# Attention scores by rows in every second unit, with P turned by the DMA and V as the matmul weights

## The chip, the cores and the metric

The kernel runs on one core of one Trainium2 chip. The metric is the time of one execution on the device in microseconds; below it is given as the median of several runs. The profile is of one further execution, taken by the hardware profiler.

## What is computed

One transformer layer over 2048 tokens of width 512: a modulated layer norm, attention with 32 query heads over 8 cached key/value heads (2048 keys, head size 128, four query heads to a key head), an output projection with a gate, and then a gMLP block with a spatial mixing matrix. The part that matters here is the attention:

```python
q = (x @ wq).reshape(B, Sq, Hq, Dh).transpose(0, 2, 1, 3)
k = jnp.repeat(k_cache, rep, axis=1)
v = jnp.repeat(v_cache, rep, axis=1)
scores = jnp.einsum('bhqd,bhkd->bhqk', q, k) * Dh ** (-0.5)
p = softmax(scores, axis=-1)
o = jnp.einsum('bhqk,bhkd->bhqd', p, v)
return o.transpose(0, 2, 1, 3).reshape(B, Sq, Hq * Dh) @ wo
```

The block after it computes `z = gelu(h @ w_in)`, normalises its second half, mixes it over tokens with `w_sp`, multiplies with the first half and projects with `w_out`.

## The kernel before

**Units.** The attention is cut into 128 units. A unit is one key head (a group `g`) and one tile of 128 queries, with the four query heads of that group together: 512 query rows against 2048 keys. There are 8 groups of 16 units. The order of all work is written out by hand: the main loop runs over iterations `it`, each of 8 slots, and in iteration `it` the scores of unit `it`, P times V of unit `it - 1` and the output projection of unit `it - 3` are interleaved slot by slot. A piece of work can be hung on a slot with `at(it, slot, fn)`, and the query projections are spread over slots through the dictionary `fill`. Each engine runs its instructions in the order in which this loop emits them.

**Scores by columns (`qk`, line 965).** A slot takes two blocks of 128 keys. For each, a block of transposed keys is the weight of the matmul, and the 512 query rows are streamed, so the scores come out with keys on the partitions and queries along the free axis. Two such matmuls of 512 columns fill one tile `s_ps` (two PSUM banks; there are two such tiles). One ScalarE instruction takes the exponential of the 1024 columns and writes bf16 into `pTs[u]`, which already is P transposed. No maximum is subtracted; a range check on the reciprocals in `rall` at the end guards a second, general path.

**P times V (`pv`, line 987).** For each query head and each of 16 key blocks the tile of P transposed (128 x 128) is the weight, and V with a column of ones beside it (129 columns) is streamed. So a unit has 64 matmuls of 129 columns, and the column of ones gives the sum of the row. After two heads VectorE takes the reciprocal (line 1006) and multiplies it in (line 1007, `onorm`). At the end of the unit SyncE's queue issues a DMA transpose of `onorm` into `oT` (line 1015), two iterations ahead of the output projection that reads it.

**Output projection and query projection.** `wo_proj` (line 1019) has four matmuls of 512 columns per unit and adds the result to an accumulator `xacc` on VectorE. `qproj` (line 928) has 16 matmuls of 512 columns for four units; four land in the slots of each unit.

**Loads and the rest.** GpSimd's queue loads V, `wq`, `wo`, the second part of the modulation weights (`wmod_b`, which lies in the buffer `wsp`) and `w_in` (`win_sb`). SyncE's queue issues all DMA transposes: keys of the next group (line 739), `oT`, the normalised inputs, and tiles of the spatial matrix (`load_wsp`, line 1102), of which the first 16 are spread over the attention and 48 come after it. The modulation columns and rows (`mod_cols_b`, `mod_rows`) are computed in iterations 9 and 10. After the last unit come the gMLP's projections (lines 1182 and 1221), the spatial mix (line 1336) and the last projection (line 1357).

Of the kernel before, what the change touches and what calls it, by code (L numbers as in the profile page):

```python
# [575 lines left out]
def kernel(  # L576
# [76 lines left out]
    mv2 = res.tile([P, NT, nc.vector.BN_AGGR_DIM], FP32, name="mv2")  # L653
    mvz = res.tile([P, NT, nc.vector.BN_AGGR_DIM], FP32, name="mvz")
    mhalf = res.tile([P, CT], FP32, name="mhalf")
    win_sb = res.tile([P, NDT, F], BF16, name="win_sb")
    wmod_a = res.tile([P, NDT, 2 * D], BF16, name="wmod_a")
    wmod_b = wspp.tile([P, NDT * 4 * D], BF16, name="wsp")[:].rearrange(
        "p (k n) -> p k n", k=NDT
    )  # L660
# [3 lines left out]
    def bank(name):  # L664
        return psum.tile([P, 512], FP32, name=name)
# [259 lines left out]
        )  # L925
    warm(2)

    def qproj(b, heads, c0, n):

        g, ch = divmod(b, NCH)  # L930
        if b not in qTs:
            qTs[b] = early.tile([P, REP, 512], BF16, name="qT")
        one = n * len(heads) <= 512
        ps = {}

        def mm(hh, dt):
            if dt == 0 and (not one or hh == heads[0]):
                ps[0] = bank("misc")
            o0 = (hh - heads[0]) * n if one else 0
            nc.tensor.matmul(  # L940
                ps[0][:, o0 : o0 + n],
                lhsT=wqs[g][:, dt, hh * DH : (hh + 1) * DH],
                rhs=hTs[ch][:, dt, c0 : c0 + n],
                start=(dt == 0),
                stop=(dt == NDT - 1),
            )
            if dt == NDT - 1 and (not one or hh == heads[-1]):
                hs = heads if one else [hh]
                dst = qTs[b][:, hs[0] : hs[-1] + 1, c0 : c0 + n]
                src = ps[0][:, 0 : len(hs) * n].rearrange("p (h q) -> p h q", q=n)  # L950
                nc.vector.tensor_copy(out=dst, in_=src)  # L951

        return [lambda hh=hh, dt=dt: mm(hh, dt) for hh in heads for dt in range(NDT)]
# [2 lines left out]


    NU = HKV * NT
    pTs, onorms, oTs, xaccs, o_pss, h2Ts = {}, {}, {}, {}, {}, {}
    later = {}  # L960

    def at(it, slot, fn):
# [2 lines left out]
    def qk(u, i):  # L965
        g, j = divmod(u, NT)
        b, jj = g * NCH + j // CT, j % CT
        if i == 0:
            pTs[u] = late.tile([P, NKT, 512], BF16, name="pT")
        s_ps = bank2()  # L970
        for h in range(2):
            kt = 2 * i + h
            nc.tensor.matmul(  # L973
                s_ps[:, h * 512 : (h + 1) * 512].rearrange("p (r q) -> p r q", r=REP),
                lhsT=groups[g]["kT"][:, kt * P : (kt + 1) * P],
                rhs=qTs[b][:, :, jj * P : (jj + 1) * P],
                start=True,
                stop=True,
            )
        nc.scalar.activation(  # L980
            out=pTs[u][:, 2 * i : 2 * i + 2, :],
            in_=s_ps[:].rearrange("p (k q) -> p k q", k=2),
            func=ACT.Exp,
            scale=inv_sqrt_dh,
        )

    def pv(u, i):
        g = u // NT
# [152 lines left out]
    ln1_at(1, (0, 7), (1, 2), (2, 2))  # L1141
    ln1_at(2, (2, 4), (3, 1), (4, 5))
    ln1_at(3, (5, 1), (5, 5), (7, 4))
    at(2, 5, lambda: nc.gpsimd.dma_start(out=wmod_b, in_=wmod_dram[:, :, 2 * D : NMOD]))
    at(5, 5, lambda: nc.gpsimd.dma_start(out=win_sb[:], in_=win_dram))
    at(9, 4, mod_cols_b)
    at(10, 4, mod_rows)

    def set_fill(b):

        fs = qproj(b, list(range(REP)), 0, 512)
        for k, fn in enumerate(fs):
            it, slot = (b - 1) * CT + k // NDT, k % NDT
            if b == 1:
                it, slot = 2 + (10 + k) // 16, (5 + k // 2) % 8
            elif b == 2:
                it, slot = (5, k // 2) if k < 8 else (it, slot)
            fill.setdefault((it, slot), []).append(fn)

    def wsp0():  # L1160
        wsp[0] = wspp.tile([P, NT, 512], BF16, name="wsp")

    at(20, 0, wsp0)
    for st in range(NT):
        at(21 + 6 * st, 2, lambda st=st: load_wsp(wsp[0], 0, st))
    for g in range(1, HKV):
        it = (g - 1) * NT
        at(it + 7, 6, lambda g=g: load_k(g))
        at(it + 8, 3, lambda g=g: load_v(g))
        at(it + 9, 3, lambda g=g: load_wo(g, nc.gpsimd))  # L1170
        at(it + 7, 3, lambda g=g: load_wq(g, nc.gpsimd))


    zs = {}
# [81 lines left out]
    for ch in range(3):  # L1256
        at(NU + 5, 5 + ch, lambda ch=ch: z2_norm(ch))

    for it in range(NU + 6):
        if it < NU:  # L1260
            if it % CT == 0 and it // CT + 1 < NB:
                set_fill(it // CT + 1)
        elif it == NU:
            free_a.close()
            z2p = fast.enter_context(tc.tile_pool(name="z2p", bufs=1))
            zs["z2"] = z2p.tile([P, NT, FH], BF16, name="z2")
        wf = wo_proj(it - 3) if 3 <= it < NU + 3 else []
        for i in range(NSLOT):
            for fn in later.pop((it, i), []):
                fn()  # L1270
            if it < NU:
                qk(it, i)
            if 1 <= it <= NU:
                pv(it - 1, i)
            for fn in fill.pop((it, i), []):
                fn()
            if i >= 4 and wf:
                wf[i - 4]()
            if it >= NU:
                zrun(3)  # L1280
        if 3 <= it < NU + 3 and it - 3 >= (HKV - 1) * NT:
            ln2(it, (it - 3) % NT)
        if it == NU + 2:
            free_b.close()
            mlp = fast.enter_context(tc.tile_pool(name="mlp", bufs=1, side="right"))
# [170 lines left out]
```

## Time and profile before

| | |
|---|---|
| median of 10 runs | 1321.15 us (1320.66 to 1321.62) |
| the profiled execution, its own time | 1320.8 us |
| span of its profile | 1319.0 us |
| TensorE busy | 1311.5 us (99%) |
| ScalarE busy | 1077.7 us (82%) |
| VectorE busy | 471.7 us (36%) |
| attention units | about us 11 to 1144 of the span |
| after the units | about us 1144 to 1319 |

Busy time of an engine is the time in which at least one of its instructions is in progress. TensorE's matmuls overlap one another in their pipeline, so the mean duration of one matmul is longer than the distance between two, and what a matmul costs is read from the distance between starts. ScalarE's instructions can overlap a little too. The span is what the profiler saw of the instructions; the 1.8 us between it and the execution's own time lie around it.

### The profile page before, as it was taken

To read this page: it belongs to the slowest core of one execution; us is meant where nothing else is said; L and a number is where in the kernel's file an instruction comes from. 1 tells how busy PE (TensorE), PEld (TensorE's weight loads), DVE (VectorE), ACT (ScalarE), POOL (GpSimd) and SP (SyncE) were. 2 spreads that over 40 slices of the span, in tenths; PEclk is the share of its full clock that TensorE was granted. 3 is DMA by queue.
4 is the path that set the end of the run, shared out by engine and by line. 5 is a ranking of instruction groups with operands and counts; after the bars stand their busy time and mean duration, and the time that the engine had idled before them with its cause. 6 is when DMAs were issued, how large, how long until landed. Compare 5 with 4: busy or idle time off the path is not lost.

```text
span 1319.0 us, 27930 instructions
## 1 busy us (share of the span) xinstructions
PE 1311.5 (99%) x12359; PEld 858.3 (65%) x12359; DVE 471.7 (36%) x1162; ACT 1077.7 (82%) x1061; POOL 51.9 (4%) x96
## 2 busy tenths in 40 slices
PE   9999999999999999999999999999999999999998
PEld 5666666666666666666666666666666666644445
DVE  6532222222222222222222222222222566794444
ACT  7898999999999999999999999999999999650000
POOL 1201000000000000000000000000000000020000
PEclk9999999999999999999999999999999999999999
DMA  6542121112101111211110211121101122143300
GB/s 180 152 93 45 28 39 37 37 17 50 37 17 37 30 37 37 33 33 38 33 38 13 53 38 33 17 53 26 29 13 21 25 32 32 33 115 81 69 20 26
DMA packets 148944, 58.64 MB, mean 44 GB/s; under 512 B 138480, under 2 KB 144880, under 8 KB 148816
## 3 DMA queue, kind: packets, MB, share of 16 engines
q1 hardware_dynamic: 141792, 37.65, 15.5%
q0 software_dynamic: 4432, 16.91, 4.6%
q8 instruction: 98, 1.61, 0.5%
q10 hardware_dynamic: 2592, 2.23, 0.5%
q14 instruction: 30, 0.25, 0.1%
HBM read 21.89 MB, written 2.10 MB: 18 GB/s over the span
## 4 chain that ended last, share of the span: by engine, by line
PE 99%; DMA 0%; DVE 0%; ACT 0%; issue 0%; DVEq 0%
PE o_ps L995 35%; PE s_ps L973 33%; PE misc L1027 8%; PE misc L940 8%; PE misc L1336 7%; PE s_ps L1182 2%; PE s_ps L1221 2%; PE o_ps L1357 1%; PE s_ps L1357 1%; DMA wmod_a<-in_w_mod_dram 0%; PE misc L850 0%; PE o_ps L781 0%; DVE hT L809 0%; PE misc L1344 0%; ACT pT L980 0%; DVE tmp L1369 0%
## 5 line engine op out<-in xcount | busy, mean ns | idle before, releaser
L980 ACT ACTIVATE pT<-s_ps 128x1024 bf16<-128x1024 f32 x1024 | 1044.4, 1025 | 81.3 <-PE s_ps L973 7.1
L995 PEld LDWEIGHTS <-pT 128*128 128x128 bf16 x8192 | 548.5, 98 | 241.2
L995 PE MATMUL o_ps<-v,pT 128*128 128x129 bf16 x8192 | 631.4, 220 | 0.0
L973 PE MATMUL s_ps<-qT,kT 128*128 128x512 bf16 x2048 | 608.9, 379 | 0.3 <-ACT pT L980 0.2
L1006 DVE RECIPROCAL rall<-o_ps 128x2 f32<-128x2 f32 x256 | 43.7, 171 | 743.7 <-PE o_ps L995 740.4
L973 PEld LDWEIGHTS <-kT 128*128 128x128 bf16 x2048 | 199.3, 98 | 119.2 <-issue 0.8
L1027 PE MATMUL misc<-wo_g,oT 128*128 128x512 bf16 x512 | 194.0, 379 | 0.0
L940 PE MATMUL misc<-hT,wq_g 128*128 128x512 bf16 (+2 forms) x528 | 190.7, 371 | 0.1
L1007 DVE TENSOR_TENSOR onorm<-o_ps,rall 128x256 bf16<-128x256 f32 x256 | 108.7, 425 | 8.8
L1336 PE MATMUL misc<-wsp,z 128*128 128x512 bf16 (+2 forms) x560 | 100.7, 336 | 0.0
L951 DVE CAST qT<-misc 128x512 bf16<-128x512 f32 x127 | 86.4, 681 | 2.0 <-PE misc L940 2.0
L1336 PEld LDWEIGHTS <-z 128*128 128x128 bf16 x560 | 50.6, 98 | 48.5
L1040 DVE TENSOR_TENSOR xacc<-misc,xacc 128x512 f32<-128x512 f32 x112 | 76.2, 680 | 0.0
L940 PEld LDWEIGHTS <-wq_g 128*128 128x128 bf16 x528 | 50.4, 98 | 1.2 <-issue 0.4
L1027 PEld LDWEIGHTS <-oT 128*128 128x128 bf16 x512 | 50.1, 98 | 0.9
L1351 DVE TENSOR_TENSOR gb<-misc,bsp_bc 128x512 bf16<-128x512 f32 (+1 forms) x28 | 18.4, 658 | 58.3 <-PE misc L1336 58.3
L1182 PE MATMUL s_ps<-win_sb,hT 128*128 128x448 bf16 x128 | 27.0, 352 | 0.0
L1192 ACT ACTIVATE z<-s_ps 128x896 bf16<-128x896 f32 x16 | 14.7, 917 | 14.9 <-PE s_ps L1182 14.9
L1221 PE MATMUL s_ps<-hT,win_sb 128*128 128x512 bf16 x112 | 24.5, 379 | 0.0
L1229 ACT ACTIVATE z1T<-s_ps 128x1024 bf16<-128x1024 f32 x14 | 14.3, 1024 | 10.1 <-PE s_ps L1221 9.1
L692 DVE BATCH_NORM_STATS2 bnst<-x_sb 128x6 f32<-128x512 bf16 x32 | 21.9, 683 | 1.3 <-DMA x_sb<-in_A_x_dram 0.8
L1357 PE MATMUL o_ps<-wout_sb,yT 128*128 128x512 bf16 x84 | 20.1, 379 | 0.0
(88 smaller groups left out, 268.7 us busy)
## 6 DMA issues: line engine op xcount, KB each, us to landing
wq_g<-in_A_wq_dram POOLq DMA_DIRECT2D x7, 512.0 KB, 4.0
v<-in_A_v_cache_dram POOLq DMA_DIRECT2D x7, 512.0 KB, 5.9
wo_g<-in_A_wo_dram POOLq DMA_DIRECT2D x7, 512.0 KB, 4.7
oT<-onorm SPq DMA_TRANSPOSE x128, 2.4
wsp<-in_w_mod_dram POOLq DMA_DIRECT2D x1, 2048.0 KB, 8.8
out_dram<-yout ACTq DMA_DIRECT2D x16, 128.0 KB, 1.7
win_sb<-in_B_w_in_dram POOLq DMA_DIRECT2D x1, 1792.0 KB, 7.7
x_sb<-in_A_x_dram SPq DMA_DIRECT2D x3, 512.0 KB, 5.4
```

Source lines behind the costliest of these rows:

```text
L940: nc.tensor.matmul(ps[0][:, o0 : o0 + n], lhsT=wqs[g][:, dt, hh * DH : (hh + 1) * DH], rhs=hTs[ch][:, dt, c0 : c0 + n], start=(dt == 0), s ...
L951: nc.vector.tensor_copy(out=dst, in_=src)
L973: nc.tensor.matmul(s_ps[:, h * 512 : (h + 1) * 512].rearrange("p (r q) -> p r q", r=REP), lhsT=groups[g]["kT"][:, kt * P : (kt + 1) * P], ...
L980: nc.scalar.activation(out=pTs[u][:, 2 * i : 2 * i + 2, :], in_=s_ps[:].rearrange("p (k q) -> p k q", k=2), func=ACT.Exp, scale=inv_sqrt_dh,)
L995: nc.tensor.matmul(o_ps[:, hh % 2, 0 : DH + 1], lhsT=pTs[u][:, kt, hh * P : (hh + 1) * P], rhs=groups[g]["v1"][:, kt, 0 : DH + 1], start=( ...
L1007: nc.vector.tensor_tensor(out=onorms[u][:, hh - 1 : hh + 1, :], in0=o_ps[:, :, 0:DH], in1=rall[:, c0 : c0 + 2].unsqueeze(2).to_broadcast([ ...
L1027: nc.tensor.matmul(X_ps[:], lhsT=oTs[u][:, hh, :], rhs=groups[g]["wo"][:, hh, :], start=(hh == 0), stop=(hh == REP - 1),)
L1040: nc.vector.tensor_tensor(out=xaccs[j][:], in0=X_ps[:], in1=xaccs[j][:], op=ALU.add)
L1182: nc.tensor.matmul(ps[0][:, hf * 512 : hf * 512 + FC], lhsT=h2Ts[j // CT][:, dt, (j % CT) * P : (j % CT + 1) * P], rhs=win_sb[:, dt, FH + ...
L1221: nc.tensor.matmul(ps[0][:, k * 512 : (k + 1) * 512], lhsT=win_sb[:, dt, f * P : (f + 1) * P], rhs=h2Ts[2 * ch2 + k][:, dt, :], start=(dt ...
L1336: nc.tensor.matmul(g_ps[:, :n], lhsT=z2[:, st, f * P : (f + 1) * P], rhs=wsp[t][:, st, c0 : c0 + n], start=(st == 0), stop=(st == NT - 1 a ...
L1357: nc.tensor.matmul(dst, lhsT=yT[:, f, jj * P : (jj + 1) * P], rhs=wout_sb[:, f, :], start=(f == 0), stop=(f == NFT - 1),)
```

## The change

A unit is now of one of two kinds. `by_rows(u)` is true for every second unit from 6 to 110, and for units 112, 116 and 120: 56 units. The other 72 are as before.

In a unit by rows, a slot takes half of one query head: the transposed queries of the head are the weight, and two times 512 keys are streamed, so the scores have queries on the partitions. ScalarE's exponential also gives out the sum of its 1024 columns (`accum_out`). Two slots after a head is complete, `turn_rows` adds the two sums, takes the reciprocal, multiplies the 128 x 2048 tile of P by it in place, and SyncE's queue issues one DMA transpose of that tile (512 KB) into `pTs[u]`. P by rows lies in the buffers `win_sb` (three heads) and `wmod_a` (the fourth). P times V of such a unit (`pv_rows`) has a block of V as the weight and 512 columns of P transposed streamed, 16 matmuls, whose result already is `oT` and is copied there by VectorE. It comes three iterations after the scores (five in the last group) instead of one. The output projection follows two iterations later, as before.

There are three buffers for P transposed instead of two; the third is `wsp`. So `wmod_b`, which lay in it, is loaded and used earlier (iterations 2, 4 and 5), `win_sb` is loaded in iteration 123, and the first 16 tiles of the spatial matrix are loaded in iterations 129 to 132. Iteration 7 has no P times V, and takes the whole query projection of units 8 to 11; iteration 125 has two. The loads for the next group move to later slots.

```diff
-    win_sb = res.tile([P, NDT, F], BF16, name="win_sb")
+    win_t = res.tile([P, NDT * F], BF16, name="win_sb")
+    win_sb = win_t[:].rearrange("p (k f) -> p k f", k=NDT)
...
+    pn = [win_t[:, r * SK : (r + 1) * SK] for r in range(REP - 1)]
+    pn.append(wmod_a[:].rearrange("p k n -> p (k n)")[:, 0:SK])
...
+    TURN_A, TURN_B = CT + 2, (HKV - 1) * NT
+    def by_rows(u):
+        return u % 2 == 0 if TURN_A <= u < TURN_B else u % 4 == 0 and TURN_B <= u < NU - CT
+    def pv_at(u):
+        return u + 1 if not by_rows(u) else u + 3 if u < TURN_B else u + 5
+    users, homes = dict(pT0=-2, pT1=-1, wsp=TURN_A), {}
+    for u in range(NU):
+        homes[u] = min(users, key=lambda k: users[k])
+        assert users[homes[u]] < u
+        users[homes[u]] = pv_at(u)
...
         s_ps = bank2()
+        if by_rows(u):
+            hh, half = divmod(i, 2)
+            for c in range(2):
+                k0 = (2 * half + c) * 512
+                nc.tensor.matmul(
+                    s_ps[:, c * 512 : (c + 1) * 512],
+                    lhsT=qTs[b][:, hh, jj * P : (jj + 1) * P],
+                    rhs=groups[g]["kT"][:, k0 : k0 + 512],
+                    start=True,
+                    stop=True,
+                )
+            nc.scalar.activation(
+                out=pn[hh][:, half * HK : (half + 1) * HK],
+                in_=s_ps[:],
+                func=ACT.Exp,
+                scale=inv_sqrt_dh,
+                accum_out=rsums[u][:, i : i + 1],
+            )
+            if half == 1:
+                at(*divmod(u * NSLOT + i + 2, NSLOT), lambda: turn_rows(u, hh))
+            return
...
+    def turn_rows(u, hh):
...
+        nc.vector.tensor_tensor(
+            out=tot[:], in0=rs[:, 2 * hh : 2 * hh + 1], in1=rs[:, 2 * hh + 1 : 2 * hh + 2], op=ALU.add
+        )
+        nc.vector.reciprocal(out=rinv, in_=tot[:])
+        nc.vector.tensor_scalar(
+            out=pn[hh], in0=pn[hh], scalar1=rinv, scalar2=None, op0=ALU.mult
+        )
+        nc.sync.dma_start_transpose(
+            out=pTs[u][:, :, hh * P : (hh + 1) * P], in_=pn[hh]
+        )
+    def pv_rows(u, i, n):
...
+        for kt in range(i * NKT // n, (i + 1) * NKT // n):
+            nc.tensor.matmul(
+                o_pss[u][:],
+                lhsT=groups[g]["v1"][:, kt, 0:DH],
+                rhs=pTs[u][:, kt, :],
+                start=(kt == 0),
+                stop=(kt == NKT - 1),
+            )
+        if i == n - 1:
+            oTs[u] = late.tile([P, REP, P], BF16, name="oT", bufs=3)
+            nc.vector.tensor_copy(
+                out=oTs[u][:], in_=o_pss[u][:].rearrange("p (r q) -> p r q", r=REP)
+            )
...
-    at(2, 5, lambda: nc.gpsimd.dma_start(out=wmod_b, in_=wmod_dram[:, :, 2 * D : NMOD]))
-    at(5, 5, lambda: nc.gpsimd.dma_start(out=win_sb[:], in_=win_dram))
-    at(9, 4, mod_cols_b)
-    at(10, 4, mod_rows)
+    at(2, 1, lambda: nc.gpsimd.dma_start(out=wmod_b, in_=wmod_dram[:, :, 2 * D : NMOD]))
+    at(NU - CT - 1, 2, lambda: nc.gpsimd.dma_start(out=win_sb, in_=win_dram))
+    at(4, 4, mod_cols_b)
+    at(5, 4, mod_rows)
...
+        hole = TURN_A + 1 if (TURN_A + 1) // CT == b - 1 else None
+        fs = qproj(b, list(range(REP)), 0, 512, ("misc", "o_ps" if hole else "misc"))
...
+            if hole:
+                it, slot = divmod(hole * NSLOT + k // 2 - 1, NSLOT)
...
-    at(20, 0, wsp0)
+    at(NU + 1, 0, wsp0)
     for st in range(NT):
-        at(21 + 6 * st, 2, lambda st=st: load_wsp(wsp[0], 0, st))
+        at(NU + 1 + st // 4, 2 * (st % 4), lambda st=st: load_wsp(wsp[0], 0, st))
     for g in range(1, HKV):
         it = (g - 1) * NT
-        at(it + 7, 6, lambda g=g: load_k(g))
-        at(it + 8, 3, lambda g=g: load_v(g))
-        at(it + 9, 3, lambda g=g: load_wo(g, nc.gpsimd))
-        at(it + 7, 3, lambda g=g: load_wq(g, nc.gpsimd))
+        at(it + 7, 4, lambda g=g: load_wq(g, nc.gpsimd))
+        at(it + 9, 5, lambda g=g: load_k(g))
+        at(it + 11, 4, lambda g=g: load_v(g))
+        at(it + 13, 4, lambda g=g: load_wo(g, nc.gpsimd))
...
-        wf = wo_proj(it - 3) if 3 <= it < NU + 3 else []
+        pvs = [u for u in (it - 5, it - 3, it - 1) if 0 <= u < NU and pv_at(u) == it]
+        wos = [u for u in (it - 7, it - 5, it - 3) if 0 <= u < NU and pv_at(u) + 2 == it]
+        wf = [fn for u in wos for fn in wo_proj(u)]
...
-            if 1 <= it <= NU:
-                pv(it - 1, i)
+            if len(pvs) == 1:
+                pv_part(pvs[0], i, NSLOT)
+            elif pvs:
+                n = NSLOT // 2
+                pv_part(pvs[i // n], i % n, n)
```

## The prediction

> **What bounds the kernel now.** I start from the busy shares and the slices, since they say which engine to look at and whether the stages differ.
>
> ```profile
> PE 1311.5 (99%) x12359; PEld 858.3 (65%) x12359; DVE 471.7 (36%) x1162; ACT 1077.7 (82%) x1061; POOL 51.9 (4%) x96
> ACT 7898999999999999999999999999999999650000
> DMA  6542121112101111211110211121101122143300
> ```
>
> TensorE (PE) is busy all the time, ScalarE (ACT) almost so during the units. Busy alone doesn't name the bound, so next the chain of work that ended last, and its pieces around us 601.
>
> ```profile
> PE 99%; DMA 0%; DVE 0%; ACT 0%; issue 0%; DVEq 0%
> 601.51 0.43 PE s_ps L973 x2
> 601.94 0.45 PE o_ps L995 x8
> 602.39 0.21 PE misc L940
> 602.61 0.43 PE s_ps L973 x2
> ```
>
> The chain never leaves PE: a slot takes 1.10 us, of which 0.43 are scores, 0.45 P times V and 0.21 a projection, with no gap. So the time is the number of matmuls times the distance between them. The timelines of SyncE's queue and of PE give these distances.
>
> ```profile
> 311.42 45.21 SPq L1015 DMA_TRANSPOSE oT<-onorm  x6
> 417.10 45.21 SPq L1015 DMA_TRANSPOSE oT<-onorm  x6
> 1237.59 10.53 PE L1336 MATMUL misc<-wsp,z 128*128 128x512 bf16 x48
> 1247.96 0.81 PE L1357 MATMUL o_ps<-wout_sb,yT 128*128 128x512 bf16 x3
> ```
>
> Twelve units lie between the first two starts: 105.68 / 12 = 8.81 us a unit. In the other two, 48 matmuls of 512 columns take 10.37 us: 0.216 each. A unit has 24 of those (5.18 us), which leaves 3.62 us for the 64 of P times V: 56.6 ns each.
>
> The other question is how far ACT is from being the bound.
>
> ```profile
> L980 ACT ACTIVATE pT<-s_ps 128x1024 bf16<-128x1024 f32 x1024 | 1044.4, 1025 | 81.3 <-PE s_ps L973 7.1
> L980 ACT ACTIVATE pT<-s_ps x5: 1017/1030/1055, 1120.0 to 1123.6; 128x1024 bf16<-128x1024 f32 x5
> L768 ACT ACTIVATE en<-c_f x1: 205/205/205, 2.9 to 2.9; 128x4 f32<-128x4 f32 x1
> 1119.32 0.59 PE L973 MATMUL s_ps<-qT,kT 128*128 128x512 bf16 x2
> ```
>
> An exponential lasts 1.025 us. The second line is ACT asked about us 1120 to 1124.5, where slots hold no projection: five starts in 3.6 us, one every 0.90. So two can overlap by some 0.12 us, and ACT needs about 0.91 us a slot where PE needs 1.10. The last line gives the slack in time: the scores begin at 1119.32, their exponential at 1120.0 (0.68 later), it ends 1.03 later, and the same one of two tiles is refilled two slots (2.20) after 1119.32. So ACT may run about 0.45 us late before PE waits.
>
> **What the Trainium skill says.** "TensorE: Matmul & The Clock Gate", section "Wait — 56ns, not 53.3ns?": a warm matmul costs its columns at 2.4 GHz plus about 2.5 ns. The trace agrees: 215.8 ns by the page against 216, and 56.3 for 129 columns against 56.6. "ScalarE: Activation LUTs", section "What ACT_TABLE_LOAD costs": back-to-back ACTIVATEs overlap by about 93 ns (0.12 here), and a [128,1] pointer operand adds about 93 ns; no page prices the accumulator output. "DMA: Bandwidth & Descriptors", section "Latency and other measured facts": DMA transposes reach 261 GB/s in strided form; this trace is lower, about 185 (below).
>
> **The change part by part.**
>
> *P times V on PE.* A unit by rows replaces 64 matmuls of 129 columns (3.62 us) by 16 of 512 (16 x 0.216 = 3.46). That is 0.165 us a unit by the trace and 0.147 by the skill's formula; times 56 units, 9.2 or 8.2 us. I take 9. The scores keep 16 matmuls of 512 columns. All of this is on the chain.
>
> *ACT with a sum.* The trace shows no accumulator output. Lower bound: nothing, 0.91 us a slot. Upper bound: the sum is read out by one more small instruction that doesn't overlap, as long as the 128x4 one, 1.025 + 0.205 = 1.23. In between, an added 0.093 (my choice, an estimate from the skill's price of a [128,1] operand) and one or two more semaphore waits of 17 ns: about 1.03. That is under PE's 1.10, so it costs nothing; what hides it is PE. Late starts are also absorbed: a unit by rows may lose 0.45 us, and the following unit by columns wins 8 x (1.08 - 0.91) back. PE begins to wait at 1.10 + 0.45 / 8 = 1.156 a slot, and the gain is used up at 1.177.
>
> *VectorE (DVE).* Per unit by rows it loses two pairs of reciprocal and product (2 x (0.17 + 0.425) = 1.2 us) and gets four times a small sum and reciprocal (0.17 each) and the product over 2048 columns. The same operation took 417 ns for 512 and 505 for 896 columns, so 0.77 for 2048. With the copy of 512 columns (0.68): 4 x 1.1 + 0.7 - 1.2 = +3.9. Two units have 17.5 us and DVE is now 27% busy in us 300 to 400, so about half. In the last group it is 53% busy, but only one unit in four is by rows. Nothing on the chain; two o_ps and two misc banks cover a delay of about 1 us.
>
> *DMA.* Four transposes of 512 KB for two units, and one oT less.
>
> ```profile
> q1 hardware_dynamic: 141792, 37.65, 15.5%
> DMA to landing us min/median/max: 4.4/4.5/6.1
> ```
>
> The queue that holds all transposes used 15.5% of 1319 us for 37.65 MB: 5.4 us a MB, mostly transposes. Two units then need 4 x 0.52 + 0.13 = 2.23 MB, 12 us of 17.4. The second line is the nearest row, keys of 512 KB (line 739): 4.5 us to landing. Their issue takes 1.4 to 2.6 us on SyncE's queue, so 4 of them and an oT take at most 11.6 of 17.4. Deadlines: the last head is turned in slot 1 of the next unit and read 15 slots (16 us) later; the buffer of a head is rewritten 13 slots (14 us) after its turn. Both are over 1.1 us of DVE plus 4.5 plus a queue of three. Behind these wait the oT of the unit by columns (13 us of slack) and the next keys (60 us). PE's first matmul of such a P times V gets two more waits of 51 ns; where the trace has such a wait (us 160.5) the chain shows no gap, since PE's queue is ahead. I take zero, at most 56 x 0.1 = 5.6 us.
>
> *The loads and the hole.* PE's work is only moved. wmod_b took 8.8 us to land and has some 20 us before iteration 4, slot 4. win_sb took 7.7 and has five units. The 16 tiles of the spatial matrix take about 1.26 us each of SyncE's queue in iterations 129 to 132, and the last normalised input can wait behind a few of them; they are needed only at us 1190, and the second set 24 us later. Iterations 4 to 7 are thin on PE: units 4 and 5 run some slots at ACT's 0.91 instead of 0.885, and unit 6 is by rows with almost no projection, 8 x 1.03 = 8.2 us against 7.9. I put 0.5 us on this.
>
> **The sum.** 9 - 0.5 = 8.5 us off the profiled execution's 1320.8 us (span 1319.0 plus 1.8 around it): 1312.3. The median of the runs is 0.35 above that execution, so 1312.6. Bounds of this case: a gain of 6 to 10.5 us, 1310.5 to 1315.
>
> **The rivals.**
>
> *ACT becomes the bound in units by rows.* For it: no row of the trace has the accumulator, and ACT is at 93% in us 300 to 400. Against it: much of these 93% is overlap that ACT has not had to use. At 1.23 us a slot a unit by rows falls 8 x 0.13 = 1.04 us behind, of which 0.45 is absorbed; 0.59 x 56 = 33 us, less 8.5: 1345.7, **slower**. Between 1.177 and 1.23 it ends between no change and this. I give 0.25.
>
> *The transposes become the bound.* If one takes more than (17.4 - 0.7) / 4 = 4.2 us of all engines instead of 2.8, two units last as long as their transposes. At 4.5, the landing time of the keys taken as pure throughput, two units take 18.7: 53 x 1.3 = 69 us more than now, about 1389. Against it: in the stage after the units, transposes of 128 KB that land after 2.7 us are issued every 1.26, so they overlap. 0.05.
>
> *The gain is eaten.* The extra waits show on PE (5.6 us) and unit 6 or the last group lose another us or two: 1318.5 to 1323.8. 0.06 for staying within 0.2% (2.6 us, about what a measurement of this kernel can tell from no change).
>
> That the change doesn't do what it says can be left out: in the built program PE has 2688 matmuls fewer, which is 56 x 48.
>
> **How the numbers follow.** The likeliest case has 0.64, ACT 0.25, the transposes 0.05, no change 0.06. I predict 1312.6 us. The range starts at 1310 and takes in the ACT rival up to its upper bound, 1346; what is left out is a little of ACT and the transposes. Faster 0.64, same 0.06, slower 0.30.
>
> **What would show it.** Right: the rows of P times V are 16 per unit with 0.43 us for two, the chain stays on PE at 99%, two units take 17.4 us instead of 17.6, and ACT starts in units by rows are 1.10 apart with PE as the releaser. Wrong: ACT in the chain, or starts more than 1.16 apart; an idle PE before the first matmul of `pv_rows` with the DMA as releaser; a transpose of P that lands after more than 10 us.

## The result, and the profile after

The changed kernel takes **1330.21 us** (median of 9 runs, 1328.61 to 1335.34) against 1321.02 for the kernel before beside it (30 runs, 1320.47 to 1321.62). The ratio is 1.0077 [1.0068, 1.0085]: 9 us slower, where 8.5 us faster was forecast. The profiled execution took 1328.57 us, with a span of 1326.7, so the two spans lie 7.7 us apart.

From the page of the kernel after: the busy shares, the DMA slices, the queue of the transposes, the chain by engine, and one group (busy us, mean ns, idle before).

```profile
PE 1308.9 (99%) x9671; PEld 744.4 (56%) x9671; DVE 679.4 (51%) x1666; ACT 1110.6 (84%) x1509; POOL 53.4 (4%) x96
...
DMA  8299888888787888878787879887875453264300
...
q1 hardware_dynamic: 577248, 147.77, 65.9%
...
PE 94%; DVE 3%; DMA 2%; POOL 0%; issue 0%; SPq 0%; ACT 0%; DVEq 0%; ACTq 0%; POOLq 0%
...
L1042 DVE TENSOR_SCALAR win_sb<-win_sb,rall 128x2048 bf16<-128x2048 bf16 x168 | 127.0, 756 | 6.3 <-DVE rall L1041 0.5
```

TensorE (PE) has 2688 matmuls fewer, yet is busy for only 2.6 us less. The longer matmuls that replace the short ones were forecast to save 9 us, so some 6 us of busy time came from elsewhere; part of it is that a matmul at half clock counts as busy too. The chain, 99% on PE before, now runs 2% through the DMA and 3% through VectorE (DVE). The second slice of the DMA row fell from 5 to 2, and those after it rose, most of them from 1 or 2 to 7 to 9.

**The steady stage did what was forecast.** VectorE copies one `oT` per pair of units. Two of these copies, 45 pairs apart, in its timeline (start, us, engine, line):

```profile
215.69 0.69 DVE L1064 CAST oT<-o_ps 128x512 bf16<-128x512 f32 x1 [3.41 <-PE o_ps L1055]
1000.49 0.69 DVE L1064 CAST oT<-o_ps 128x512 bf16<-128x512 f32 x1 [3.41 <-PE o_ps L1055]
```

784.80 / 45 = 17.44 us a pair, the 17.4 of the forecast, where two units took 17.61 (2 x 105.68 / 12, from the two lines of SyncE's queue in the prediction). With 56 units by rows that is 0.17 x 56 = 9.5 us gained. ScalarE (ACT) in a unit by rows, where PE happens to be ahead of it (ACT's timeline):

```profile
68.17 1.02 ACT L1008 ACTIVATE win_sb<-s_ps 128x1024 bf16<-128x1024 f32 x1
69.08 0.20 ACT L1008 ACTIVATION_READ_ACCUMULATOR win_sb<-s_ps 128x1 f32 x1
69.17 1.02 ACT L1008 ACTIVATE win_sb<-s_ps 128x1024 bf16<-128x1024 f32 x1
```

The sum is read out by an instruction of its own, 0.195 us on average, but it overlaps the exponentials on both sides: starts are 1.00 us apart, 0.09 more than the 0.91 of the kernel before. That is close to the forecast's middle value of 1.03, and it stays under PE's 1.10.

**The loss is in the first 110 us.** PE's largest waits of the kernel after (what PE had to start, what it waited for, then us in total, times, longest):

```profile
PE s_ps L1020 <- ACT wmod_a L1008: 4.0, 1, 4.0
PE misc L944 <- DVE hT L813: 3.2, 1, 3.2
PE misc L1108 <- DMA oT<-onorm: 2.7, 1, 2.7
PE o_ps L785 <- DVE onorm L767: 1.2, 1, 1.2
```

The fourth stood in the kernel before as well, with the same 1.2 us. The other three are new, and each happens once. The same kernel by stretches (us, then busy and count of PE, PEld, DVE, ACT and POOL, the granted clock, the DMA share, GB/s):

```profile
20.00:40.00 20.00, 16.75 (x178) 12.01 (x176) 10.06 (x27) 15.20 (x17) 2.19 (x3) 1.00 0.56 140
90.00:100.00 10.00, 5.36 (x34) 3.16 (x35) 2.27 (x6) 1.78 (x3) 0.00 (x0) 0.79 1.15 236
100.00:110.00 10.00, 9.50 (x32) 3.72 (x32) 1.77 (x4) 7.39 (x11) 0.00 (x0) 0.70 1.13 188
```

Here the busy share misleads: PE is 95% busy in us 100 to 110 but does 32 matmuls of 512 columns, where 46 would fit at 0.216 us each, because its clock fell after the two waits. "TensorE: Matmul & The Clock Gate" of the Trainium skill (Part 1) says that an idle window of about 3.4 us halves the clock; the trace agrees after the 4.0 us wait, with 0.85 us for two matmuls of 512 columns instead of 0.43. But the clock was also halved from about us 92.5 to 96, after a wait of only 2.7 us, and it stayed at 1.00 after the 3.2 us wait for `hT`. So in this trace the length of a wait near 3 us doesn't settle whether the clock falls. The lost clock of these 20 us, 10 x 0.21 + 10 x 0.30, is at most 5.1 us, since part of it falls into the wait itself. So 3.2 + 2.7 + 4.0 and up to 5.1 make up to 15 us. The spans call for 9.5 + 7.7 = 17.2. The rest, 2 us or more, isn't itemised; 1.2 of it came after the last unit.

**How the stall at us 96 came about.** GpSimd's and then SyncE's queue in the timelines of the kernel after:

```profile
63.57 0.83 POOL L1180 DMA_DIRECT2D mod<-modc  x1
72.50 0.58 POOL L1181 DMA_DIRECT2D ga_rows<-mod  x1 [8.10 <-DMA mod<-modc]
73.06 0.76 POOL L1180 DMA_DIRECT2D mod<-modc  x1
84.42 0.55 POOL L1181 DMA_DIRECT2D gb_rows<-mod  x1 [10.60 <-DMA mod<-modc]
84.96 0.76 POOL L720 DMA_DIRECT2D wq_g<-in_A_wq_dram  x1
```

```profile
70.61 13.84 SPq L1045 DMA_TRANSPOSE pT<-win_sb  x3
84.56 1.21 SPq L1096 DMA_TRANSPOSE oT<-onorm  x1
85.87 6.21 SPq L1045 DMA_TRANSPOSE pT<-wmod_a  x1
92.25 12.12 SPq L1045 DMA_TRANSPOSE wsp<-win_sb  x3
...
115.22 8.14 SPq L1045 DMA_TRANSPOSE pT<-win_sb  x3
```

`mod_rows` writes 512 values of 4 bytes to DRAM (line 1180), each to a place of its own, and reads them back to all partitions, twice. GpSimd waits 8.1 and 10.6 us for the two writes of 2 KB each to land. Beside them three transposes of P take 13.84 us of SyncE's queue; undisturbed ones take about 8 (the last line). The fourth head's transpose is queued behind them, and so its buffer `wmod_a` comes free late. That is the stall in the chain of waits (start, us, what):

```profile
85.78 0.09 PE o_ps L1076 x2
85.87 13.37 DMA pT<-wmod_a
...
99.34 0.07 ACT wmod_a L1008
...
100.50 1.01 PE s_ps L1020 x2
```

The transpose lands 13.37 us after its issue, the exponential of the next unit by rows waits to overwrite `wmod_a`, and PE waits for the exponential.

### The profile page after: what moved, and what is told of

The parts are those of the page before. It is cut to its first block, busy times and chain, and to the rows that moved or that the text cites. A ratio compares the mean times of both kernels' runs of the same rounds, so it can differ in the third digit from the quotient of the medians.

```text
span 1326.7 us, 24732 instructions
## 1 busy us (share of the span) xinstructions
PE 1308.9 (99%) x9671; PEld 744.4 (56%) x9671; DVE 679.4 (51%) x1666; ACT 1110.6 (84%) x1509; POOL 53.4 (4%) x96
## 3 DMA queue, kind: packets, MB, share of 16 engines
q1 hardware_dynamic: 577248, 147.77, 65.9%
q8 instruction: 78, 1.28, 0.4%
## 4 chain that ended last, share of the span: by engine, by line
PE 94%; DVE 3%; DMA 2%; POOL 0%; issue 0%; SPq 0%; ACT 0%; DVEq 0%; ACTq 0%; POOLq 0%
PE o_ps L1076 19%; PE s_ps L1020 19%; PE o_ps L1055 15%; PE s_ps L1001 14%; PE misc L944 8%; PE misc L1108 8%; PE misc L1431 7%; PE o_ps L1452 1%; DMA pT<-wmod_a 1%; DVE stz L1287 1%; DMA xnT<-xn 1%; PE o_ps L785 1%; PE s_ps L1452 1%; DMA hT<-xn 0%; PE s_ps L1265 0%
## 5 line engine op out<-in xcount | busy, mean ns | idle before, releaser
L1027 ACT ACTIVATE pT<-s_ps 128x1024 bf16<-128x1024 f32 x560 | 569.3, 1025 | 37.0 <-PE s_ps L1020 14.0
L1076 PEld LDWEIGHTS <-pT 128*128 128x128 bf16 x4480 | 300.2, 98 | 131.9 <-issue 1.1
L1008 ACT ACTIVATE win_sb<-s_ps 128x1024 bf16<-128x1024 f32 x336 | 343.9, 1024 | 10.0 <-PE s_ps L1001 3.4
L1020 PE MATMUL s_ps<-qT,kT 128*128 128x512 bf16 x1152 | 343.7, 380 | 4.3 <-ACT wmod_a L1008 4.0
L1076 PE MATMUL o_ps<-v,pT 128*128 128x129 bf16 x4480 | 345.2, 220 | 0.0
L1001 PE MATMUL s_ps<-kT,qT 128*128 128x512 bf16 x896 | 267.4, 380 | 0.2 <-ACT win_sb L1008 0.2
L1055 PE MATMUL o_ps<-pT,v 128*128 128x512 bf16 x448 | 134.4, 382 | 0.0
L1055 PE MATMUL o_ps<-wsp,v 128*128 128x512 bf16 x448 | 132.6, 379 | 0.0
L1042 DVE TENSOR_SCALAR win_sb<-win_sb,rall 128x2048 bf16<-128x2048 bf16 x168 | 127.0, 756 | 6.3 <-DVE rall L1041 0.5
L1008 ACT ACTIVATE wmod_a<-s_ps 128x1024 bf16<-128x1024 f32 x112 | 114.7, 1024 | 6.2 <-DMA pT<-wmod_a 6.2
```

Source lines behind the costliest of these rows:

```text
L1001: nc.tensor.matmul(s_ps[:, c * 512 : (c + 1) * 512], lhsT=qTs[b][:, hh, jj * P : (jj + 1) * P], rhs=groups[g]["kT"][:, k0 : k0 + 512], sta ...
L1008: nc.scalar.activation(out=pn[hh][:, half * HK : (half + 1) * HK], in_=s_ps[:], func=ACT.Exp, scale=inv_sqrt_dh, accum_out=rsums[u][:, i : ...
L1020: nc.tensor.matmul(s_ps[:, h * 512 : (h + 1) * 512].rearrange("p (r q) -> p r q", r=REP), lhsT=groups[g]["kT"][:, kt * P : (kt + 1) * P], ...
L1027: nc.scalar.activation(out=pTs[u][:, 2 * i : 2 * i + 2, :], in_=s_ps[:].rearrange("p (k q) -> p k q", k=2), func=ACT.Exp, scale=inv_sqrt_dh,)
L1042: nc.vector.tensor_scalar(out=pn[hh], in0=pn[hh], scalar1=rinv, scalar2=None, op0=ALU.mult)
L1055: nc.tensor.matmul(o_pss[u][:], lhsT=groups[g]["v1"][:, kt, 0:DH], rhs=pTs[u][:, kt, :], start=(kt == 0), stop=(kt == NKT - 1),)
```

## The experiments

Two theories, both about the early loads. **W**: `wmod_b` (2 MB, in the buffer `wsp`) is issued at us 22.97 instead of 37.21, just ahead of transposes of `hT`. **S**: the small writes of `mod_rows`, moved from iteration 10 to 5, stand beside the first transposes of P. The rival to S is **B**: the loads of a group (`wq`, V, `wo`) come in a bunch (us 84.96 to 87.01), because GpSimd's queue waited for the small writes. A further rival is that units by rows are slow in themselves. The lines behind W, each time first of the kernel before and then of the kernel after: GpSimd's queue, and the transposes of `hT` in us 20 to 40 with their median us to landing:

```profile
37.21 0.95 POOL L1144 DMA_DIRECT2D wsp<-in_w_mod_dram  x1
22.97 0.96 POOL L1225 DMA_DIRECT2D wsp<-in_w_mod_dram  x1
...
hT<-xn SPq DMA_TRANSPOSE x6, 3.7
hT<-xn SPq DMA_TRANSPOSE x4, 8.7
```

**1. `wmod_b` later.** Its load goes back to slot 5.

```diff
-    at(2, 1, lambda: nc.gpsimd.dma_start(out=wmod_b, in_=wmod_dram[:, :, 2 * D : NMOD]))
+    at(2, 5, lambda: nc.gpsimd.dma_start(out=wmod_b, in_=wmod_dram[:, :, 2 * D : NMOD]))
```

> The changed kernel with one line put back: the load of wmod_b is emitted in slot 5 of iteration 2 again, behind the layer norm operations that GpSimd waits for, instead of slot 1. Theory (collision): the 2 MB load, which GpSimd issued at us 23.0 instead of 37.2, takes the DMA engines from the four transposes of hT that PE needs at us 33; with the load behind them the 3.2 us of idle PE between us 30 and 40 are gone and nothing else changes: 1330.2 - 3.2 = 1327.0 us. Rival: hT is late because of the transposes themselves, and the time stays at 1330.

1328.33 us (1324.71 to 1331.29), ratio to before 1.0054 [1.0035, 1.0072]. The load is issued at us 37.11 again, the wait for `hT` is gone, and PE is busy for 20.00 of the 20 us from 20 to 40. But the medians differ by only 1.9 us, and the intervals of the two ratios overlap: the later stall was longer in this kernel (6.1 for `wmod_a` and 4.3 for `oT`, against 4.0 and 2.7). W is real, but it isn't the main loss.

**2. Rows without small writes.** The two rows of gates are made on PE, by eight matmuls with a broadcast vector (`sc_bc`, made in iteration 4; not shown) as weight, and nothing goes through DRAM: neither the two small writes nor the two reads behind them.

```diff
...
-            line = dram.tile([D], FP32, name=f"mod{part}")
-            nc.gpsimd.dma_start(out=line[:].rearrange("(dt p) -> p dt", p=P), in_=modc[:, cols])
-            nc.gpsimd.dma_start(out=rows[:], in_=line[:].partition_broadcast(P))
...
+            for kt in range(NDT):
+                nc.tensor.matmul(
+                    mr_ps[:],
+                    lhsT=sc_bc[:, kt, :],
+                    rhs=wmod_b[:, kt, w0 : w0 + D],
+                    start=(kt == 0),
+                    stop=(kt == NDT - 1),
+                )
+            nc.vector.tensor_copy(out=rows[:], in_=mr_ps[:])
```

> The changed kernel with the gate rows ga_rows and gb_rows computed directly as rows, by 8 matmuls of 512 columns with a broadcast weight, so that the two writes of 512 single 4-byte values to DRAM and the two broadcast reads behind them don't exist. Theory A (small writes): they hold the DMA engines around us 73 to 84, when the first unit by rows wants its four transposes; without them those land on time, PE's idle times around us 88 and 96 and the low clock after them are gone, 12.4 us less and 0.9 us of matmuls more: 1318.7 us. Rival B (burst): the 1.5 MB of wq, v and wo of the next group, which GpSimd issues back to back, are the cause; they now come earlier, and a stall of the same size remains at another place: 1326 to 1331.

1318.44 us (1316.15 to 1319.65), ratio 0.9977 [0.9967, 0.9986]: 11.8 us less than after. Of the three new waits only the one for `hT` is left (2.8 us). The group's loads now come in a bunch at us 64.88 to 67.94, the transposes beside them take 11.68 us, and PE doesn't wait there.

**3. Both.**

> Both edits of the two kernels before together. Theory: their gains add, 1330.2 - 3.2 - 11.5 = 1315.5 us, and the span before us 216 is within 2 us of that of the kernel before, at the same unit and with the deferred P times V counted. Rival: the two are the same wait seen twice, and this is no better than the better of the two.

1314.07 us (1313.06 to 1314.68), ratio 0.9942 [0.9925, 0.9959]: 16.1 us less than after. With the small writes out of the way, the later `wmod_b` is worth 4.4 us: 2.8 us of wait, and a clock that in run 2 fell to 0.50 in us 36 to 38 behind that wait. No new wait over 0.5 us is left.

**4. Small writes kept, loads held back.** This tells S from B: GpSimd waits for a row sum of a later unit ahead of each load of the first group.

```diff
+    at(10, 0, lambda: hold(8))
+    at(11, 4, lambda: hold(9))
+    at(13, 4, lambda: hold(11))
...
-        at(it + 7, 4, lambda g=g: load_wq(g, nc.gpsimd))
+        at(it + (7 if g > 1 else 10), 4, lambda g=g: load_wq(g, nc.gpsimd))
```

> The changed kernel with the small writes kept, but GpSimd made to wait, by a tiny operation on a reciprocal that VectorE has just made, before each of the three loads of group 1: wq goes out in iteration 8, v in 10 and wo in 12 instead of all three at us 85 to 87. Rival B (burst): the transposes at us 86 to 99 land on time and 11 us are won: 1319. Theory A (small writes): the transposes are late already at us 84, and at most a part is won: 1324 to 1330.

1327.89 us (1319.82 to 1330.19), ratio 1.0036 [1.0011, 1.0060]. SyncE's queue, and then PE's waits from us 60 to 125:

```profile
70.02 14.41 SPq L1045 DMA_TRANSPOSE pT<-win_sb  x3
```

```profile
PE s_ps L1020 <- ACT wmod_a L1008: 4.4, 1, 4.4
PE misc L1108 <- DMA oT<-onorm: 2.7, 1, 2.7
```

V and `wo` are now issued only after us 112, though `wq` still goes out at us 86.62, and in this execution PE's two waits are as they were. So the bunch of B isn't needed for them. What it adds stays open: the medians differ by 2.3 us and the intervals of the two ratios leave 1 to 10, single executions ran from 1319.82 to 1330.19 us, and the clock fell less here (0.95 and 0.88 in us 90 to 110, where the kernel after has 0.79 and 0.70).

**5. Small writes put back elsewhere.** Kernel 3 with two extra writes of the same form, to a place that nothing reads, at iterations 40 and 42.

```diff
+    def small(u, k):
+        hold(u)
+        line = dram.tile([D], FP32, name=f"extra{k}")
+        nc.gpsimd.dma_start(out=line[:].rearrange("(dt p) -> p dt", p=P), in_=modc[:, 0:NDT])
+    at(40, 4, lambda: small(39, 0))
+    at(42, 4, lambda: small(41, 1))
```

> The kernel with both edits (wmod_b late, gate rows by matmuls), plus two of the small writes alone, 512 single 4-byte values to a spare DRAM tensor each, held back by a tiny GpSimd operation until iterations 40 and 42, in the middle of the units. Theory A: while one of them is in flight, for some 10 us, the transposes of P beside it hardly move; SyncE's queue needs about 15 us instead of 8 for three of them, and a transpose lands after 10 us or more instead of 5. In the steady stage the buffers leave about 8 us of slack, so PE loses 0 to 5 us: 1314 to 1319. Rival: a small write only waits itself and the transposes beside it land after 5 us as ever; the time is 1314 and SyncE's queue shows nothing.

1326.00 us (1323.63 to 1331.05), ratio 1.0040 [1.0021, 1.0060]: 12 us more than kernel 3, where at most 5 was expected. Beside the first write three transposes took 12.87 us of the queue instead of 7.54, and PE lost nothing. Beside the second they took 20.95, PE waited 8.3 us, and its clock fell to 0.54. But the holds had done more than intended: V and `wo` of the next group were caught behind the second and issued right after it. So this run doesn't tell S from B, and runs 10 to 12 take that up.

**6. No units by rows.** `by_rows` returns False; every other edit of the change stays.

```diff
-        return u % 2 == 0 if TURN_A <= u < TURN_B else u % 4 == 0 and TURN_B <= u < NU - CT
+        return False
```

> The changed kernel with no unit by rows (all 128 by columns), so only its other parts: earlier wmod_b, small writes in iteration 5, later win_sb and spatial tiles, later loads, the third buffer. Theory: without the transposes of P there is nothing for the small writes to delay that PE needs; only the 3 us of late hT remain: 1321.2 + 3 = 1324, with PE busy from us 60 to 200. Rival: the moved loads alone stall PE around us 90 as in the changed kernel: 1332 or more.

1325.35 us (1324.66 to 1326.34), ratio 1.0031 [1.0018, 1.0044]. The wait for `hT` is there (3.3 us), the stall at us 96 isn't, although the small writes are. So everything that was moved costs about 4 us by itself, mostly by W; the small writes hurt only where transposes of P stand beside them.

**7. Two exponentials a slot.** Kernel 3, with the exponential of a slot of a unit by rows cut in two halves of 512 columns, each with its sum. This measures how far ACT may be late before PE waits.

```diff
-                out=pn[hh][:, half * HK : (half + 1) * HK],
-                in_=s_ps[:],
...
+            for e, w in enumerate((512, 512)):
+                nc.scalar.activation(
+                    out=pn[hh][:, half * HK + c : half * HK + c + w],
+                    in_=s_ps[:, c : c + w],
...
+                c += w
```

> The kernel with both edits, with each exponential of the units by rows cut into two of 512 columns, each with its own sum, so twice as many read-outs of the accumulator and twice the fixed cost (VectorE adds one more small sum a head). From the trace of the changed kernel: an ACTIVATE of 1024 takes 1.024 us, a read-out 0.195, and starts are 1.00 apart when ACT doesn't wait, so each pair overlaps by 0.22. For 512 columns 0.60 + 0.195 - 0.22 = 0.57, twice that is 1.15 us a slot against PE's 1.10. The prediction's rule (0.45 us may be lost in a unit by rows, and the next unit wins it back) says no loss up to 1.156: 1314 to 1317 us. Rival: no such cover, every unit by rows lasts 8 x 1.15 = 9.2 us instead of 8.8 and the time is 1314 + 56 x 0.4 = 1336.

1325.42 us (1324.84 to 1326.13), ratio 1.0032 [1.0019, 1.0044], between the two expectations. Two copies of `oT` in DVE's timeline:

```profile
609.71 0.69 DVE L1070 CAST oT<-o_ps 128x512 bf16<-128x512 f32 x1 [3.41 <-PE o_ps L1061]
627.34 0.69 DVE L1070 CAST oT<-o_ps 128x512 bf16<-128x512 f32 x1 [3.41 <-PE o_ps L1061]
```

17.63 us a pair, 0.19 more than 17.44, and 0.19 x 56 = 10.7 is the 11.4 us by which it is slower. Halves start 0.57 us apart, so a slot takes 1.14: a unit falls 8 x 0.04 = 0.32 us behind PE, and 0.19 of that is lost. By this sum the cover is 0.13 us, not 0.45; an error of 0.01 us in a slot shifts it by 0.08.

**8. First unit by rows at 10.** Kernel 1 (small writes kept, `wmod_b` late), with the first unit by rows at 10 instead of 6, after the writes have landed. The query projection that iteration 7 took goes back to earlier slots, and the empty iteration is 11. This is also the candidate for a better version.

```diff
-    TURN_A, TURN_B = CT + 2, (HKV - 1) * NT
+    TURN_A, TURN_B = CT + 6, (HKV - 1) * NT
...
+            elif b == 2:
+                it, slot = (5, k // 2) if k < 8 else (it, slot)
```

> The changed kernel with wmod_b late, the small writes kept, and the first unit by rows at 10 instead of 6 (54 units by rows; the iteration without P times V is 11, and the query projection of units 8 to 11 has its old slots). Theory A: the small writes and the loads of group 1 are through by about us 93, before the first transpose of P at about us 103, so the stall is gone without taking the writes away: 1314.1 + 0.3 for two units fewer - 0.9 of matmuls = 1313.5 us. Rival: the first units by rows stall wherever they stand (filling of the new buffers and queues): 1324 to 1328.

**1312.39 us** (1312.03 to 1313.27), ratio 0.9934 [0.9917, 0.9951]: no other kernel is faster, and it is 8.9 us under the kernel before, with two units by rows fewer than the changed kernel. Its only PE wait over 0.6 us is the 1.2 us that the kernel before had too. The loads of the group go out at us 83.69 to 85.73 and the first transpose of P at us 102.19, so this run takes the writes and the bunch out of the way together.

**9. Three exponentials a slot.** As 7, cut in 512, 256 and 256.

> This is e3_both with the exponential of each slot of a row unit cut in three (512, 256 and 256 columns, each with its sum). The kernel with two took 17.63 us a pair against 17.44, 0.19 lost a unit, at starts 1.14 us a slot. Estimate: a third piece adds another 0.15, 1.29 a slot. A cover of 0.13 us, as read from two pieces: 8 x 0.19 = 1.52 behind, 1.4 lost a unit, 56 x 1.4 = 78 us over e3_both, about 1392. With the prediction's cover of 0.45 us it would be 56 x 1.07 = 60 us, about 1374. If the added piece costs only the 0.04 that separates 1.14 from 1.10: under 1345.

1392.33 us (1391.74 to 1394.64), ratio 1.0543 [1.0526, 1.0561]. The expectation of 1392 is met. The copies of `oT` are 18.84 us apart, 1.40 more than 17.44, and a slot takes ACT 1.28 us (613.63 to 614.91): 8 x 0.18 = 1.44 behind, so here the cover is only 0.04 us. Together with run 7 that is about 0.1, far from 0.45. ACT would thus have become the bound soon above 1.10 a slot, and there each 0.01 us a slot costs 56 x 0.08 = 4.5 us.

**10. Lone writes.** Kernel 8 with three extra writes. `small` is that of run 5 with the layout in DRAM and the number of values per partition as arguments: 512 pieces of 4 bytes, then the same 2 KB as 128 pieces of 16 bytes, then 128 pieces of 4 bytes.

```diff
+    at(54, 4, lambda: small(53, 0, "(dt p) -> p dt", NDT))
+    at(70, 4, lambda: small(69, 1, "(p dt) -> p dt", NDT))
+    at(86, 4, lambda: small(85, 2, "(dt p) -> p dt", 1))
```

> This is e8_start_at_10 with three extra writes from SBUF to DRAM on GpSimd's queue, each in the quiet stretch between two groups' loads (iterations 54, 70 and 86; some us 485, 625 and 765), held until a row sum of the unit before exists: first 512 values of 4 bytes, each to a place of its own; then the same 2 KB as 128 pieces of 16 bytes; then 128 values of 4 bytes. Nothing else is moved, and no load waits behind them. Theory A (a write in many small pieces stops the transposes beside it): the first write lands after 8 to 13 us, the three transposes of that time take 11 to 14 us of SyncE's queue instead of about 7, and GB/s of that stretch falls under 60; the other two, a quarter of the pieces, land in 2 to 5 us and change the transposes by under 3 us. PE has 16 us of slack there, so the time stays within 2 us of 1312.4. Theory B (the bunch of loads was what did it): no transpose beside any of the three is over 9 us. If a write of 2 KB as such does it, the second is as slow as the first.

1340.79 us (1335.45 to 1342.37), ratio 1.0136 [1.0114, 1.0157], 28 us above kernel 8; neither theory's numbers were met. The premise was false: GpSimd's queue runs up to 160 us ahead of the loop, each load being issued as soon as its buffer is free. So the holds caught the three loads of a group each time, which were then issued within 3 us of one another, right behind the write. The next two runs take the two apart.

**11. Writes away from the loads.** The same three writes stand in the program behind the group's loads (iterations 63, 79, 95); they are issued at about us 485, 624 and 764, and no load is held.

> In e10_lone_writes GpSimd's queue ran up to 160 us ahead of the loop, so the hold before each extra write also held the next group's three loads, which then were issued together right after the write. This is the same kernel with the three writes placed in the program after those loads, where GpSimd has nothing to do for 60 us (us 485, 625, 765); it stands on e8_start_at_10, with no load moved. Theory A (a write in small pieces alone slows the transposes beside it): the first, 512 pieces of 4 bytes, lands after 8 to 13 us and the three transposes beside it take 11 to 14 us of SyncE's queue instead of about 7; the other two (128 pieces of 16 and of 4 bytes) land in 2 to 5 us and cost the transposes under 3 us; no PE idle, time within 2 us of 1312.4. Theory B (only loads that bunch do it): no transpose stretch over 9 us at any of the three, same time.

**12. The bunch alone.** Kernel 10 with the holds and without the writes.

> This is e10_lone_writes without its three writes: the holds stay, so that the loads of a group (wq, V and wo, 1.5 MB) are issued within 3 us of one another at us 485, 625 and 765, and no small write is there. Theory A (small writes do it): the three transposes beside each bunch take under 12 us, PE idle under 3 us in all, time 1312 to 1316. Theory B (the bunch does it): 18 to 25 us of SyncE's queue as in e10_lone_writes, PE waits some 5 us and more at each, its clock falls, time 1330 to 1340.

Kernel 11 takes 1312.42 us (1312.22 to 1312.72), ratio 0.9932 [0.9915, 0.9948], as kernel 8. Kernel 12 takes 1318.92 (1317.05 to 1323.91), ratio 0.9985 [0.9976, 0.9993]. SyncE's queue at the three places, first of kernel 8 (neither), then of 11 (a write alone), then of 12 (loads alone), then of 10 (a write and loads):

```profile
483.93 6.67 SPq L1045 DMA_TRANSPOSE pT<-win_sb  x3
623.45 7.32 SPq L1045 DMA_TRANSPOSE pT<-win_sb  x3
762.97 8.28 SPq L1045 DMA_TRANSPOSE pT<-win_sb  x3
```

```profile
484.12 12.73 SPq L1045 DMA_TRANSPOSE pT<-win_sb  x3
623.64 7.45 SPq L1045 DMA_TRANSPOSE pT<-win_sb  x3
763.16 12.18 SPq L1045 DMA_TRANSPOSE pT<-win_sb  x3
```

```profile
484.31 14.29 SPq L1045 DMA_TRANSPOSE pT<-win_sb  x3
623.90 18.28 SPq L1045 DMA_TRANSPOSE pT<-win_sb  x3
766.85 18.12 SPq L1045 DMA_TRANSPOSE pT<-win_sb  x3
```

```profile
483.70 28.11 SPq L1045 DMA_TRANSPOSE pT<-win_sb  x3
636.76 21.63 SPq L1045 DMA_TRANSPOSE pT<-win_sb  x3
783.35 23.41 SPq L1045 DMA_TRANSPOSE pT<-win_sb  x3
```

Each of the two stretches the transposes, and together they cost more than the sum of both at every place (21.4 us at the first, where the two alone cost 6.1 and 7.6). A write of 512 pieces of 4 bytes costs them about 6 us (12.73 against 6.67) and lands after 11.4. The same 2 KB in 128 pieces of 16 bytes costs next to nothing by itself (7.45 against 7.32, landed after 4.2). A quarter of the bytes, 128 pieces of 4, still costs 3.9 us (12.18 against 8.28, landed after 9.5); there the expectation was wrong. So it is the 4-byte pieces, not the bytes, and not in proportion to their number; each place is read from one trace. What happens in that time is seen in the stretch from us 490 to 495 of kernel 11, and then of kernel 8:

```profile
490.00:495.00 5.00, 4.95 (x24) 2.25 (x23) 1.65 (x4) 4.78 (x6) 0.00 (x0) 1.00 1.75 22
```

```profile
490.00:495.00 5.00, 4.95 (x24) 2.25 (x23) 1.50 (x3) 4.78 (x6) 0.00 (x0) 1.00 1.10 171
```

The DMA share (the last number but one; in this view it can go over 1) goes up, and the transfer rate (the last, in GB/s) falls to an eighth. One such stretch stays within the slack, and PE's clock and work are the same in both. Loads alone cost 7.6, 11.0 and 9.8 us of the queue and PE 5.3 us of waits in all, more than theory A of the expectation had and, with 1318.92 us, far less than its theory B; a write and loads together cost PE 11.8, 5.3 and 7.2 us of waits, and the clock on top.

## Why the prediction was wrong

**The step that failed is "The loads and the hole", costed at 0.5 us.** In its place the trace has up to 15 us of waits and slowed clock, and run 3, which takes both causes away, is 16.1 us faster. The working asked of each moved load only whether it would *arrive* in time. It didn't ask what the load would stand *beside*.

- *`wmod_b`.* The step took the load's landing time and its deadline, and both were fine. But it moved 14 us earlier, not the four slots that the edit suggests, because before it had been issued only behind the statistics of a later norm on GpSimd (us 36.21, then 37.21). At us 22.97 it meets the transposes of `hT`: they land after 8.7 us in the median where they took 3.7, and PE waits 3.2 us. Shown by run 1, where the wait is gone, and by run 6, where it is left alone; worth 4.4 us between runs 2 and 3.
- *`mod_rows`.* The step says that "PE's work is only moved". That this function also issues four DMAs on GpSimd, two of them in 4-byte pieces, was left out, although the kernel before has them, at iteration 10, where no transposes of P exist. Moved to iteration 5 they fall on those of unit 6. Shown by run 2 (without the writes, with the bunch of loads), run 4 (with the writes, without the bunch), run 6 (writes without transposes of P) and run 11 (the stretching by itself); run 8 fits both S and B. In run 2 this is 11.8 us, with the two reads behind the writes gone as well, which no run takes apart. The deadline that broke is one of the DMA step: it gave the buffer of a head 14 us and took 4.5 for the landing, and here a transpose landed after 13.37.
- *Why it costs more than the stretch.* One write stretches three transposes by 5 to 6 us, which the buffers absorb without a wait of PE (run 11, and the first write of run 5); a stretch of 11 us in run 12 was too much. Here there were two writes in a row, just when the first units by rows fill the four buffers of P, and behind them an `oT`, the fourth head and a group's loads. That this coincidence makes the difference is read from the trace: two writes with no load at all beside them weren't run. The waits of 2.7 and 4.0 us at the end of it also cost PE its clock.

The forecast's own list of what would prove it wrong had the sign: "a transpose of P that lands after more than 10 us". It landed after 13.37. But the rival tied to it had transposes that are too slow *throughout*, 1389 us; a burst in one place wasn't among the cases. The slower side was put on ACT instead, and by its own work ACT was never late enough in the changed kernel to hold PE for more than 0.2 us. The range holds 1330 only because its upper end, 1346, was put there for that rival: that is luck. The direction was wrong.

**What was right.** P times V: 0.165 us a unit forecast, 0.17 measured. ACT with a sum: 1.03 us a slot forecast, 1.00 measured. Here the size came out partly by luck: the 0.093 that was added is the price of another operand, while the trace shows the separate instruction of the upper bound (0.195 us, where 0.205 was taken), most of it overlapped. The transposes of P land after 5.1 us in the median (4.3 for the fourth head) where 4.5 was taken, and in the steady stage PE doesn't wait for them. VectorE: the product over 2048 columns took 0.756 us for 0.77, the small sum and the reciprocal 0.155 and 0.164 for 0.17, and the copy 0.69 for 0.68; none of it was on the path. With both early causes gone and hardly another edit, kernel 8 takes 1312.4 us where the forecast had 1312.6; it has two units by rows fewer, so the agreement is worth a few tenths at most.

**What was mis-sized without harm.** The cover of a late ACT was put at 0.45 us; runs 7 and 9 give 0.13 and 0.04. The 0.45 was read at one place where slots hold no projection; why it isn't there in the units wasn't tried. At ACT's real 1.00 it made no difference, but at the upper bound of 1.23 the rival would have cost 56 x (1.04 - 0.13) = 51 us or a little more, not 33. The DMA queue needs 5.9 us a MB (65.9% of 1326.7 us for 147.77 MB), not 5.4, and in the steady stage the DMA is busy 7 to 9 tenths of the time, not 7. That leaves little room for anything else.

**What stays open.** About 2 us of the loss isn't itemised. Why kernel 3 is 1.7 us slower than kernel 8, wasn't tried; its eight matmuls of 512 columns for the rows (8 x 0.216 = 1.7 us, less the small ones that they replace) are a candidate, and kernel 3 has a wait of 0.5 us that kernel 8 hasn't. How much of the 11.8 us the loads behind the writes added isn't shown. What in the DMA engines makes 4-byte pieces hold up the transposes isn't shown by any run; only that they do.

## What to carry to other kernels

When a change moves a load or a function to another place, list every DMA that it issues, and for each queue ask what it will be running beside, not only whether the data arrives in time; an edit of a few slots can move a transfer by many microseconds, when the queue that issues it was held by something else. When a change fills the DMA from 1 or 2 tenths to 8, each transfer that was harmless before has to be looked at again, small scattered writes and bunches of loads first; where they can't be made otherwise, start the new scheme after them. A one-time stall in the first tenth of a kernel can eat what a thousand microseconds of steady gain bring in, so compare waits and clock stretch by stretch before the mechanism itself is blamed.

## What the runs showed of the hardware that was not expected

- A DRAM write of 512 values of 4 bytes from 128 partitions lands after some 9 to 12 us, and DMA transposes beside it nearly stand still (22 GB/s instead of 171 over 5 us) while the DMA counts as busier (1.75 against 1.10). The same 2 KB in 16-byte pieces lands in 4.2 us and left three transposes beside it at 7.45 us, where 7.32 is undisturbed.
- Three loads of 512 KB within 3 us of one another stretch three transposes from about 7 to 14 to 18 us; where the loads go out one by one, as in kernel 8 from us 388 to 603, three transposes take 6.7 to 7.6 us.
- The sum of an exponential is read out by an instruction of its own (195 ns), of which only some 0.09 us is added to the distance between two exponentials of 1024 columns.
- After waits of PE of 2.7 to 3.2 us the clock sometimes fell to half (2.7 in the changed kernel, 2.8 in run 2) and sometimes stayed at 1.00 (2.7 in run 4, 2.9 in run 12, 3.2 in the changed kernel). After the waits of 4.0 and 4.4 us in the changed kernel and run 4 it fell.
